# Work of the weight-decode stage moved from GpSimd to VectorE and ScalarE

## The chip, the cores and the metric

The kernel runs on one core of one Trainium2 chip. Its engines are TensorE (PE in the profile, with its weight loads as PEld), VectorE (DVE), ScalarE (ACT), GpSimd (POOL) and SyncE (SP), which issues the DMAs. The metric is the device time of one execution in microseconds, taken as the median of several runs; lower is better.

## What is computed

Windowed attention over 8 batches, 8 heads, 576 positions and a head size of 64, followed by a feed-forward layer whose activation is a rational function. The inputs are float32, except the two weight matrices, which are float64.

```
scores = q @ k.T / 8, kept where 0 <= pos_q - pos_k < 64, else -1e9
attn   = exp(scores - max) / (sum + 1e-9)
x      = attn @ v                      # 4608 tokens x 512
h      = x @ w_in                      # 512 x 2048
P      = a0 + a1*h + a2*h^2 + a3*h^3
Q      = 1 + |b0|*|h| + |b1|*h^2
out    = (P / (Q + 1e-6)) @ w_out      # 2048 x 512
```

The weights reach the kernel as pairs of 32-bit words (a low and a high word). The kernel makes float32 numbers of them itself.

## The kernel before

**Precision.** Each operand of the feed-forward matmuls is split into a high part in a reduced format (fp32r) and a low part, the rest. A product is then three matmuls: high x low, low x high, high x high. For every operand there is thus a cast for the high part and a subtraction for the low part.

**Weights.** `decode` (L101) handles one block of 128 x 512 numbers, and there are 16 blocks of `w_in` and 16 of `w_out`. It loads the word pairs into the landing buffer `w_st` (two buffers), then works in `w_c` (two buffers): L113 removes the sign of the high word (a bitwise and), L114 clamps from below, L116 shifts and masks, L117 joins the low word's upper bits, L118 joins the sign. These five run on VectorE. ScalarE casts the result to the high part (L121), and GpSimd subtracts to get the low part (L122).

**Attention.** A chunk is 384 tokens, and there are 12. For each chunk four units (one per pair of heads) run: `unit_load`, `unit_scores` (matmuls L182, mask and scale on VectorE L188 or L192, row maximum L198, six exponentials on ScalarE L201, sums and reciprocal L203 and L204, and the multiplication of all 128 x 768 numbers by the reciprocals, L205, on GpSimd), `unit_transpose` and `unit_av`, which splits the result into `xh` (ScalarE) and `xl` (VectorE, L229).

**Feed-forward.** `ffn1` (L234) does one step: 12 matmuls into the PSUM tile `h` (two buffers), then the gate, one rational function on 128 x 384 numbers. ScalarE takes |h| (L244) and a3*h + a2 (L245); VectorE makes the numerator (L246, L247); GpSimd makes the denominator less one, first the scaling u = |b1|*|h| + |b0| (L248), then the product with |h| (L249); ScalarE takes a logarithm and an exponential for the reciprocal (L251, L252); VectorE refines it and multiplies (L253 to L255); ScalarE casts to the high part `gh` (L258); the low part `gl` (L260) is a subtraction, on GpSimd for the first 20 gates (`GLN`) and on VectorE after that. `ffn2` (L270) follows three steps later with 9 matmuls.

**Order.** There are 192 steps. The first 32 are chunks 0 and 1 in halves: the first eight blocks of columns for chunk 0, then for chunk 1, then the other eight for chunk 1 and for chunk 0. The decodes are spread over the prologue and steps 0 to 22 (L304 to L315), so that a weight block is decoded some steps ahead of its use. From step 32 on each chunk takes 16 steps and no weights are decoded. The four units of chunk 2 are issued at steps 21 to 28 in the program, the eight of chunks 0 and 1 ahead of that. A planner that simulates the engines then puts the instructions of each engine into their final order, so an instruction can run well ahead of its step in the program. Each engine works its queue in order.

Of the kernel before, what the change touches and what calls it, by code (L numbers as in the profile page):

```python
# [9 lines left out]
F32 = mybir.dt.float32  # L10
F32R = mybir.dt.float32r
U32 = mybir.dt.uint32
AF = mybir.ActivationFunctionType
ALU = mybir.AluOpType
# [3 lines left out]
CH = 384  # L18
TC = CH // WIN
PR = TC // 2  # L20
GLN = 20
AHEAD = 3
LAG = 3
W_AT = 0, 1, 2, 3
# [7 lines left out]
def swa_rational_ffn(ctx: ExitStack, tc: tile.TileContext, qT, kT, v, w_in, w_out, a, b, out):  # L32
    nc = tc.nc
    P = 128
# [18 lines left out]
    op = ctx.enter_context(tc.tile_pool(name="op", bufs=2))  # L53
# [28 lines left out]
    b_sb = const.tile([P, 2], F32, name="b_sb")  # L82
# [18 lines left out]
    def decode(src, hi, lo):  # L101

        w = stage.tile([P, 512, 2], U32, name="w_st", bufs=2)
        if len(src.shape) == 3:
            nc.sync.dma_start(out=w.rearrange("p (c n) two -> p c (n two)", c=src.shape[1]), in_=src)
        else:
            nc.sync.dma_start(out=w.rearrange("p n two -> p (n two)"), in_=src)
        low, high = w[:, :, 0], w[:, :, 1]
        c = stage.tile([P, 512], U32, name="w_c")
        cf = c.bitcast(F32)  # L110


        nc.vector.tensor_scalar(out=c, in0=high, scalar1=0x7FFFFFFF, scalar2=None, op0=ALU.bitwise_and)  # L113
        nc.vector.tensor_scalar(out=cf, in0=cf, scalar1=2.0 ** -15, scalar2=None, op0=ALU.max)  # L114

        nc.vector.tensor_scalar(out=c, in0=c, scalar1=3, scalar2=0x3FFFFFF8, op0=ALU.logical_shift_left, op1=ALU.bitwise_and)  # L116
        nc.vector.scalar_tensor_tensor(out=c, in0=low, scalar=29, in1=c, op0=ALU.logical_shift_right, op1=ALU.bitwise_or)  # L117
        nc.vector.scalar_tensor_tensor(out=c, in0=high, scalar=0xC0000000, in1=c, op0=ALU.bitwise_and, op1=ALU.bitwise_or)  # L118
        if len(hi.shape) == 3:
            cf = cf.rearrange("p (c n) -> p c n", c=hi.shape[1])  # L120
        nc.scalar.copy(out=hi, in_=cf)  # L121
        nc.gpsimd.tensor_tensor(out=lo, in0=cf, in1=hi.bitcast(F32), op=ALU.subtract)  # L122

    def load_w_in(i):
        sl = slice(i * P, (i + 1) * P)
        decode(w_in_v[:, :, 2 * i * P:2 * (i + 1) * P], wi_h[:, :, sl], wi_l[:, :, sl])

    def load_w_out(i):
        decode(w_out_v[:, i, :], wo_h[:, i, :], wo_l[:, i, :])
# [42 lines left out]
    def unit_scores(c, hp):  # L172
        u = live[c, hp]

        ps = ps_a.tile([P, 2, 512], F32, name="ps_s", bufs=1)
        for p in range(PR):
            for z in range(2):
                for e in range(2):
                    j = 2 * p + e
                    k = u["kt"][z * 64:z * 64 + 64].rearrange("p t s -> p (t s)")  # L180
                    w = u["kw"][j] * WIN
                    nc.tensor.matmul(ps[e * 64:e * 64 + 64, z, p * P:(p + 1) * P], u["q"][z * 64:z * 64 + 64, j, :],  # L182
                                     k[:, w:w + P], start=True, stop=True)
        sm = att.tile([P, 2, PR * P], F32, name="sm")
        m0 = u["m0"]
        for z in range(2):
            if m0 is None:
                nc.vector.scalar_tensor_tensor(out=sm[:, z, :].rearrange("p (r c) -> p r c", c=P),  # L188
                                               in0=ps[:, z, 0:PR * P].rearrange("p (r c) -> p r c", c=P), scalar=SCALE,
                                               in1=mask[:, 1:2, :].broadcast_to([P, PR, P]), op0=ALU.mult, op1=ALU.min)  # L190
            else:
                nc.vector.scalar_tensor_tensor(out=sm[:, z, :], in0=ps[:, z, 0:PR * P], scalar=SCALE,  # L192
                                               in1=mask[:, m0:m0 + PR, :].rearrange("p r c -> p (r c)"),
                                               op0=ALU.mult, op1=ALU.min)
        sm = sm.rearrange("p z (r c) -> p (z r) c", c=P)
        NR = 2 * PR
        nmx = att.tile([P, NR], F32, name="nmx")
        nc.vector.tensor_reduce(out=nmx, in_=sm, axis=AX.X, op=ALU.max, negate=True)  # L198
        sums = att.tile([P, NR], F32, name="sums")
        for j in range(NR):  # L200
            nc.scalar.activation(sm[:, j, :], sm[:, j, :], AF.Exp, bias=nmx[:, j:j + 1], accum_out=sums[:, j:j + 1])  # L201
        rs = att.tile([P, NR], F32, name="rs")
        nc.vector.tensor_scalar(out=sums, in0=sums, scalar1=1e-9, scalar2=None, op0=ALU.add)  # L203
        nc.vector.reciprocal(out=rs, in_=sums)  # L204
        nc.gpsimd.tensor_tensor(out=sm, in0=sm, in1=rs.unsqueeze(2).broadcast_to([P, NR, P]), op=ALU.mult)  # L205
        u["sm"] = sm

    def unit_transpose(c, hp):
# [23 lines left out]
    n_gates = [0]  # L232

    def ffn1(c, i):  # L234
        h = ps_h.tile([P, CH], F32, name="h")
        n = 0
        for cc in range(NCC):
            for w, x in ((wi_h, xl), (wi_h, xh), (wi_l, xh)):
                nc.tensor.matmul(h, w[:, cc, i * P:(i + 1) * P], x[c, cc], start=n == 0, stop=n == 3 * NCC - 1)  # L239
                n += 1  # L240
        ah = tmp.tile([P, CH], F32, name="ah")
        u = tmp.tile([P, CH], F32, name="u")
        num = tmp.tile([P, CH], F32, name="num")
        nc.scalar.activation(ah, h, AF.Abs)  # L244
        nc.scalar.activation(num, h, AF.Identity, scale=a_sb[:, 3:4], bias=a_sb[:, 2:3])  # L245
        nc.vector.tensor_tensor(out=num, in0=num, in1=h, op=ALU.mult)  # L246
        nc.vector.scalar_tensor_tensor(out=num, in0=num, scalar=a_sb[:, 1:2], in1=h, op0=ALU.add, op1=ALU.mult)  # L247
        nc.gpsimd.tensor_scalar(out=u, in0=ah, scalar1=b_sb[:, 1:2], scalar2=b_sb[:, 0:1], op0=ALU.mult, op1=ALU.add)  # L248
        nc.gpsimd.tensor_tensor(out=u, in0=u, in1=ah, op=ALU.mult)  # L249

        nc.scalar.activation(ah, u, AF.Ln, bias=QADD)  # L251
        nc.scalar.activation(ah, ah, AF.Exp, scale=-1.0)  # L252
        nc.vector.scalar_tensor_tensor(out=u, in0=u, scalar=QADD, in1=ah, op0=ALU.add, op1=ALU.mult)  # L253
        nc.vector.scalar_tensor_tensor(out=u, in0=u, scalar=2.0, in1=ah, op0=ALU.subtract, op1=ALU.mult, reverse0=True)  # L254
        nc.vector.scalar_tensor_tensor(out=num, in0=num, scalar=a_sb[:, 0:1], in1=u, op0=ALU.add, op1=ALU.mult)  # L255
        gh = gp.tile([P, CH], F32R, name="gh")
        gl = gp.tile([P, CH], F32R, name="gl")
        nc.scalar.copy(out=gh, in_=num)  # L258
        n_gates[0] += 1
        (nc.gpsimd if n_gates[0] <= GLN else nc.vector).tensor_tensor(out=gl, in0=num, in1=gh.bitcast(F32), op=ALU.subtract)  # L260
        gs[c, i] = gh, gl


# [56 lines left out]
    for c, i0, i1 in phases:  # L320
        if c and c not in start:
            start[c] = s
            every = prev // NU
            for k in range(NU):
                p = max(s - prev + every * k - AHEAD, 0)
                at(p, unit_load, c, k)
                at(p, unit_scores, c, k)
                at(p + 1, unit_transpose, c, k)
                at(p + 1, unit_av, c, k)
        prev = i1 - i0  # L330
        s += prev


    for k in range(NU + 2):
        if k < NU:
            unit_load(0, k)
            unit_scores(0, k)
        if 1 <= k <= NU:
            unit_transpose(0, k - 1)
        if k >= 2:  # L340
            unit_av(0, k - 2)
        if k in W_AT:
            load_w_in(W_AT.index(k))
        if k == 1:
            load_coefficients()

    for s in range(total + LAG):
        for fn, *args in todo.get(s, ()):
            if fn in (load_w_in, load_w_out):
                fn(*args)  # L350
        if s < total:
            ffn1(*steps[s])
        for fn, *args in todo.get(s, ()):
            if fn not in (load_w_in, load_w_out):
                fn(*args)
        if s >= LAG:
            ffn2(s - LAG)
# [31 lines left out]
```

## Time and profile before

| | |
|---|---|
| median of 3 runs | 1064.74 us (1063.88 to 1066.21) |
| the profiled execution's own time | 1063.77 us |
| its span, first to last instruction | 1062.0 us |
| mean granted TensorE clock | 0.966 |
| busy: PE, DVE, ACT, POOL | 963.7, 917.7, 674.3, 525.0 us |
| weight decodes | 32, the last one ending on VectorE at 207.5 us |
| gates started by then | 17 of 192 |

Busy time is the time in which at least one instruction of an engine is under way. The profile's granted clock is the share of the full TensorE clock that the chip let through. A group of instructions is named by its line, its engine, its operation, and the tile that it writes and those that it reads. "Idle before" is the engine's idle time ahead of instructions of that group, with what ended it.

### The profile page before, as it was taken

To read this page: it belongs to the slowest core of one execution; us is meant where nothing else is said; L and a number is where in the kernel's file an instruction comes from. 1 tells how busy PE (TensorE), PEld (TensorE's weight loads), DVE (VectorE), ACT (ScalarE), POOL (GpSimd) and SP (SyncE) were. 2 spreads that over 40 slices of the span, in tenths; PEclk is the share of its full clock that TensorE was granted. 3 is DMA by queue.
4 is the path that set the end of the run, shared out by engine and by line. 5 is a ranking of instruction groups with operands and counts; after the bars stand their busy time and mean duration, and the time that the engine had idled before them with its cause. 6 is when DMAs were issued, how large, how long until landed. Compare 5 with 4: busy or idle time off the path is not lost.

```text
span 1062.0 us, 18218 instructions
## 1 busy us (share of the span) xinstructions
PE 963.7 (91%) x6624; PEld 846.0 (80%) x6624; DVE 917.7 (86%) x1583; ACT 674.3 (63%) x1702; POOL 525.0 (49%) x511
## 2 busy tenths in 40 slices
PE   2558667899999999999999999999999999999997
PEld 2446555778888888888888888888888888888996
DVE  6999989988888898898888888888888888888885
ACT  3454445467666766766766766766666667667654
POOL 5356658864454445435435535534444444454432
PEclk9778779899999999999999999999999999999999
DMA  5543343102121121110211211210211211200000
GB/s 183 173 152 93 107 130 110 35 1 73 48 66 30 59 58 32 63 61 28 70 45 29 69 48 33 92 31 28 85 29 30 88 30 32 93 16 1 31 2 30
DMA packets 68538, 64.10 MB, mean 60 GB/s; under 512 B 4448, under 2 KB 61792, under 8 KB 68448
## 3 DMA queue, kind: packets, MB, share of 16 engines
q1 hardware_dynamic: 68448, 62.93, 19.0%
q8 instruction: 52, 0.85, 0.3%
q14 instruction: 38, 0.31, 0.1%
HBM read 53.48 MB, written 9.44 MB: 59 GB/s over the span
## 4 chain that ended last, share of the span: by engine, by line
DVE 36%; ACT 20%; POOL 19%; PE 17%; issue 5%; DMA 3%; POOLq 0%; SPq 0%; DVEq 0%; ACTq 0%
PE o L280 8%; ACT sm L201 8%; POOL u L248 7%; PE h L239 7%; DVE u L253 7%; POOL u L249 6%; POOL sm L205 4%; DVE u L254 4%; DVE nmx L198 4%; DVE num L255 2%; ACT ah L251 2%; DVE w_c L117 2%; DVE gl L260 2%; ACT ah L252 2%; DVE w_c L118 2%
## 5 line engine op out<-in xcount | busy, mean ns | idle before, releaser
L239 PE MATMUL h<-xl,wi_h 128*128 128x384 f32 x768 | 269.4, 351 | 30.3 <-DVE num L247 22.3
L248 POOL TENSOR_SCALAR u<-ah,b_sb 128x384 f32<-128x384 f32 x192 | 164.6, 860 | 262.8 <-ACT ah L244 199.6
L239 PE MATMUL h<-xh,wi_h 128*128 128x384 f32 x768 | 264.3, 344 | 0.0
L239 PE MATMUL h<-xh,wi_l 128*128 128x384 f32 x768 | 263.5, 343 | 0.0
L280 PE MATMUL o<-wo_h,gl 128*128 128x512 f32 x576 | 236.8, 411 | 25.4 <-DVE gl L260 14.4
L280 PE MATMUL o<-wo_h,gh 128*128 128x512 f32 x576 | 228.6, 397 | 0.0
L280 PE MATMUL o<-wo_l,gh 128*128 128x512 f32 x576 | 228.0, 396 | 0.0
L249 POOL TENSOR_TENSOR u<-u,ah 128x384 f32<-128x384 f32 x192 | 204.5, 1071 | 9.8
L239 PEld LDWEIGHTS h<-xl,wi_h 128*128 128x128 f32 x768 | 148.2, 193 | 40.1 <-DVE num L247 26.1
L205 POOL TENSOR_TENSOR sm<-sm,rs 128x768 f32<-128x768 f32 x48 | 81.4, 1696 | 195.8 <-DVE rs L204 195.8
L201 ACT ACTIVATE sm<-sm,nmx 128x128 f32<-128x128 f32 x288 | 111.9, 390 | 102.7 <-DVE nmx L198 102.4
L260 DVE TENSOR_TENSOR gl<-num,gh 128x384 fp32r<-128x384 f32 x172 | 154.0, 899 | 13.0 <-ACT gh L258 10.0
L245 ACT ACTIVATE num<-h,a_sb 128x384 f32<-128x384 f32 x192 | 128.5, 670 | 45.7 <-DVE gl L260 35.8
L280 PEld LDWEIGHTS o<-wo_h,gl 128*128 128x128 f32 x576 | 109.6, 190 | 58.9 <-DVE gl L260 19.2
L239 PEld LDWEIGHTS h<-xh,wi_h 128*128 128x128 f32 x768 | 148.5, 193 | 4.7
L253 DVE SCALAR_TENSOR_TENSOR u<-u,ah 128x384 f32<-128x384 f32 x192 | 116.7, 608 | 40.9 <-ACT ah L252 39.2
L251 ACT ACTIVATE ah<-u 128x384 f32<-128x384 f32 x192 | 100.4, 523 | 80.2 <-POOL u L249 79.3
L239 PEld LDWEIGHTS h<-xh,wi_l 128*128 128x128 f32 x768 | 148.3, 193 | 0.0
L280 PEld LDWEIGHTS o<-wo_h,gh 128*128 128x128 f32 x576 | 109.7, 190 | 25.2
L258 ACT CAST gh<-num 128x384 fp32r<-128x384 f32 x192 | 96.7, 508 | 47.5 <-DVE num L255 47.4
L280 PEld LDWEIGHTS o<-wo_l,gh 128*128 128x128 f32 x576 | 109.9, 191 | 18.7
L255 DVE SCALAR_TENSOR_TENSOR num<-num,a_sb,u 128x384 f32<-128x384 f32 x192 | 121.1, 636 | 2.9
(45 smaller groups left out, 1274.1 us busy)
## 6 DMA issues: line engine op xcount, KB each, us to landing
out<-ob SPq DMA_DIRECT2D x33, 256.0 KB, 2.0
w_st<-w_in SPq DMA_DIRECT2D x16, 512.0 KB, 3.7
w_st<-w_out SPq DMA_DIRECT2D x16, 512.0 KB, 3.6
q<-qT SPq DMA_DIRECT2D x32, 192.0 KB, 3.4
vt<-v SPq DMA_DIRECT2D x16, 384.0 KB, 3.4
vt<-v SPq DMA_DIRECT2D x16, 320.0 KB, 3.3
kt<-kT SPq DMA_DIRECT2D x16, 224.0 KB, 3.5
kt<-kT SPq DMA_DIRECT2D x16, 192.0 KB, 3.5
```

What stands on the lines that cost most here:

```text
L201: nc.scalar.activation(sm[:, j, :], sm[:, j, :], AF.Exp, bias=nmx[:, j:j + 1], accum_out=sums[:, j:j + 1])
L205: nc.gpsimd.tensor_tensor(out=sm, in0=sm, in1=rs.unsqueeze(2).broadcast_to([P, NR, P]), op=ALU.mult)
L239: nc.tensor.matmul(h, w[:, cc, i * P:(i + 1) * P], x[c, cc], start=n == 0, stop=n == 3 * NCC - 1)
L245: nc.scalar.activation(num, h, AF.Identity, scale=a_sb[:, 3:4], bias=a_sb[:, 2:3])
L248: nc.gpsimd.tensor_scalar(out=u, in0=ah, scalar1=b_sb[:, 1:2], scalar2=b_sb[:, 0:1], op0=ALU.mult, op1=ALU.add)
L249: nc.gpsimd.tensor_tensor(out=u, in0=u, in1=ah, op=ALU.mult)
L251: nc.scalar.activation(ah, u, AF.Ln, bias=QADD)
L253: nc.vector.scalar_tensor_tensor(out=u, in0=u, scalar=QADD, in1=ah, op0=ALU.add, op1=ALU.mult)
L255: nc.vector.scalar_tensor_tensor(out=num, in0=num, scalar=a_sb[:, 0:1], in1=u, op0=ALU.add, op1=ALU.mult)
L258: nc.scalar.copy(out=gh, in_=num)
L260: (nc.gpsimd if n_gates[0] <= GLN else nc.vector).tensor_tensor(out=gl, in0=num, in1=gh.bitcast(F32), op=ALU.subtract)
L280: nc.tensor.matmul(acc[c][t], g[:, ts], w[:, i, :], start=first and n == 0, stop=last and n == 2)
```

## The change

Up to the end of decoding, and a little beyond, five kinds of work leave GpSimd: the low part of the weights goes to VectorE (L122), and so does the low part of all gates (the first 20 were on GpSimd); the scaling of the first 28 gates goes to ScalarE and their product to VectorE; the softmax multiplication of chunks 0 and 1 goes to VectorE. In return the sign removal of the decode goes from VectorE to ScalarE, as an absolute value of the high word read as a float32. Gates from the 29th on, and the softmax multiplication from chunk 2 on, stay on GpSimd.

```diff
-GLN = 20
+DEC = 28
...
-        nc.vector.tensor_scalar(out=c, in0=high, scalar1=0x7FFFFFFF, scalar2=None, op0=ALU.bitwise_and)
+        nc.scalar.activation(cf, w.bitcast(F32)[:, :, 1], AF.Abs)
...
-        nc.gpsimd.tensor_tensor(out=lo, in0=cf, in1=hi.bitcast(F32), op=ALU.subtract)
+        nc.vector.tensor_tensor(out=lo, in0=cf, in1=hi.bitcast(F32), op=ALU.subtract)
...
-        nc.gpsimd.tensor_tensor(out=sm, in0=sm, in1=rs.unsqueeze(2).broadcast_to([P, NR, P]), op=ALU.mult)
+        (nc.vector if c < 2 else nc.gpsimd).tensor_tensor(out=sm, in0=sm, in1=rs.unsqueeze(2).broadcast_to([P, NR, P]), op=ALU.mult)
...
-        nc.gpsimd.tensor_scalar(out=u, in0=ah, scalar1=b_sb[:, 1:2], scalar2=b_sb[:, 0:1], op0=ALU.mult, op1=ALU.add)
-        nc.gpsimd.tensor_tensor(out=u, in0=u, in1=ah, op=ALU.mult)
+        n_gates[0] += 1
+        if n_gates[0] <= DEC:
+            nc.scalar.activation(u, ah, AF.Identity, scale=b_sb[:, 1:2], bias=b_sb[:, 0:1])
+            nc.vector.tensor_tensor(out=u, in0=u, in1=ah, op=ALU.mult)
+        else:
+            nc.gpsimd.tensor_scalar(out=u, in0=ah, scalar1=b_sb[:, 1:2], scalar2=b_sb[:, 0:1], op0=ALU.mult, op1=ALU.add)
+            nc.gpsimd.tensor_tensor(out=u, in0=u, in1=ah, op=ALU.mult)
...
-        n_gates[0] += 1
-        (nc.gpsimd if n_gates[0] <= GLN else nc.vector).tensor_tensor(out=gl, in0=num, in1=gh.bitcast(F32), op=ALU.subtract)
+        nc.vector.tensor_tensor(out=gl, in0=num, in1=gh.bitcast(F32), op=ALU.subtract)
```

## Prediction

> **What bounds the kernel now.** I read the head of the page first, then the busy time of the engines by stretch, cut where the last weight decode ends on VectorE, then VectorE's waits, and last its groups of instructions in the decode stage.
>
> ```profile
> span 1062.0 us, 18218 instructions
> ```
>
> The last line of the last decode, from the instructions in order of time (start and duration first):
>
> ```profile
> 206.50 1.04 DVE L118 SCALAR_TENSOR_TENSOR w_c<-w_st,w_c 128x512 uint32<-128x512 uint32 x1
> ```
>
> The columns of the next view, busy time by stretch, are the length, then PE, PEld, DVE, ACT and POOL busy with counts, the granted clock, the DMA share and GB/s.
>
> ```profile
> 0.00:8.00 8.00, 1.56 (x24) 1.18 (x24) 0.00 (x0) 1.28 (x1) 6.56 (x26) 1.00 0.70 213
> 8.00:207.60 199.60, 127.87 (x861) 106.05 (x862) 189.66 (x300) 94.78 (x257) 122.97 (x93) 0.82 0.39 120
> 207.60:300.00 92.40, 89.91 (x593) 77.67 (x593) 80.97 (x136) 59.97 (x143) 46.76 (x46) 1.00 0.16 50
> 300.00:1000.00 700.00, 688.28 (x4877) 611.29 (x4876) 602.02 (x1069) 483.98 (x1235) 328.53 (x323) 1.00 0.15 47
> ```
>
> The span has two halves with different limits. From 207.6 us on TensorE is busy 97 to 98% of the time and nothing on another engine is worth much. From 8 to 207.6 us, the stage in which the 32 weight blocks are decoded, VectorE is busy 189.66 of 199.60 us and idle for only 9.94, while TensorE has 72 us to spare and ScalarE 105. GpSimd is busy 122.97 us there.
>
> ```profile
> DVE w_c L113 <- DMA w_st<-w_in: 12.7, 3, 8.1
> DVE w_c L113 <- DMA w_st<-w_out: 1.5, 2, 0.9
> DVE w_c L113 <- POOL wo_l L122: 1.4, 1, 1.4
> DVE w_c L113 <- POOL wi_l L122: 1.2, 1, 1.2
> ```
>
> These are all of VectorE's longer waits up to 207.6 us (total, times, longest); the 8.1 us is the first load. So VectorE's own queue sets the end of this stage, and the rest of the kernel follows when it lets go. The question is what its instructions cost. Its groups in the stretch 8 to 207.6 us (busy us, mean ns, idle before):
>
> ```profile
> L118 DVE SCALAR_TENSOR_TENSOR w_c<-w_st,w_c 128x512 uint32<-128x512 uint32 x32 | 33.0, 1035 | 0.1
> L117 DVE SCALAR_TENSOR_TENSOR w_c<-w_st,w_c 128x512 uint32<-128x512 uint32 x32 | 30.6, 959 | 0.3
> L114 DVE TENSOR_SCALAR w_c<-w_c 128x512 f32<-128x512 f32 x32 | 20.8, 648 | 0.3
> L116 DVE TENSOR_SCALAR w_c<-w_c 128x512 uint32<-128x512 uint32 x32 | 19.9, 621 | 0.3
> L113 DVE TENSOR_SCALAR w_c<-w_st 128x512 uint32<-128x512 uint32 x32 | 18.4, 574 | 16.7 <-DMA w_st<-w_in 12.7 <-DMA w_st<-w_out 1.5 <-POOL wo_l L122 1.4
> L253 DVE SCALAR_TENSOR_TENSOR u<-u,ah 128x384 f32<-128x384 f32 x16 | 14.2, 888 | 0.0
> L254 DVE SCALAR_TENSOR_TENSOR u<-u,ah 128x384 f32<-128x384 f32 x16 | 13.1, 830 | 0.0
> L255 DVE SCALAR_TENSOR_TENSOR num<-num,a_sb,u 128x384 f32<-128x384 f32 x16 | 11.5, 730 | 0.0
> ...
> L198 DVE TENSOR_REDUCE nmx<-sm 128x6 f32<-128x768 f32 x10 | 9.4, 942 | 0.0
> L246 DVE TENSOR_TENSOR num<-num,h 128x384 f32<-128x384 f32 x17 | 9.2, 540 | 0.0
> L192 DVE SCALAR_TENSOR_TENSOR sm<-ps_s,mask 128x384 f32<-128x384 f32 x16 | 8.1, 546 | 0.0
> ```
>
> And single instructions in order of time, VectorE's and then the one GpSimd instruction of that stretch (start, duration):
>
> ```profile
> 88.51 0.61 DVE L247 SCALAR_TENSOR_TENSOR num<-num,a_sb,h 128x384 f32<-128x384 f32 x1
> 89.03 1.14 DVE L116 TENSOR_SCALAR w_c<-w_c 128x512 uint32<-128x512 uint32 x1
> 90.09 0.55 DVE L253 SCALAR_TENSOR_TENSOR u<-u,ah 128x384 f32<-128x384 f32 x1
> 90.56 0.41 DVE L113 TENSOR_SCALAR w_c<-w_st 128x512 uint32<-128x512 uint32 x1
> 90.90 0.68 DVE L117 SCALAR_TENSOR_TENSOR w_c<-w_st,w_c 128x512 uint32<-128x512 uint32 x1
> 91.50 0.55 DVE L254 SCALAR_TENSOR_TENSOR u<-u,ah 128x384 f32<-128x384 f32 x1
> 91.97 0.41 DVE L114 TENSOR_SCALAR w_c<-w_c 128x512 f32<-128x512 f32 x1
> 92.31 0.68 DVE L118 SCALAR_TENSOR_TENSOR w_c<-w_st,w_c 128x512 uint32<-128x512 uint32 x1
> 92.91 0.60 DVE L255 SCALAR_TENSOR_TENSOR num<-num,a_sb,u 128x384 f32<-128x384 f32 x1
> ```
>
> ```profile
> 88.88 1.01 POOL L260 TENSOR_TENSOR gl<-num,gh 128x384 fp32r<-128x384 f32 x1 [1.97 <-ACT gh L258]
> ```
>
> While GpSimd runs its L260, VectorE's L116 takes 1.14 us; once GpSimd is quiet the same shape takes 0.41 (L113, L114), the two-input lines 0.68 (128x512) and 0.55 or 0.60 (128x384). The group means lie far above these. But L246 and L192, with one input in PSUM, and the reduce L198, with one input, keep 0.54, 0.55 and 0.94 us through the same stage. So the stretch comes from GpSimd, and it hits single-input scalar operations from SBUF to SBUF and operations with two inputs in SBUF. In the quiet rows the next start comes 0.07 to 0.08 us before the last end, so the net price on a full queue is 0.34 (0.41), 0.60 (0.68) and 0.47 (0.55).
>
> **The change part by part**, on VectorE's queue between 8 and 207.6 us, for the same work (32 decodes, 16 to 17 gates, 10 attention units).
>
> *What GpSimd's silence gives.* Mean minus quiet duration, per decode: L113 0.16, L114 0.24, L116 0.21, L117 0.28, L118 0.355, together 1.25 us; 32 of them are 39.9 us. Per gate: L253 0.34, L254 0.28, L255 0.13, together 0.74; 16 are 11.9. Sum 51.8 us.
>
> *What VectorE loses and gets.* The rows for the counts and the neighbours' prices:
>
> ```profile
> L121 ACT CAST wo_h<-w_c 128x512 fp32r<-128x512 f32 x16 | 9.9, 616 | 24.2 <-DVE w_c L118 24.2
> ```
>
> ```profile
> L245 ACT ACTIVATE num<-h,a_sb 128x384 f32<-128x384 f32 x17 | 11.4, 672 | 6.0 <-POOL gl L260 6.0
> ```
>
> ```profile
> L248 POOL TENSOR_SCALAR u<-ah,b_sb 128x384 f32<-128x384 f32 x17 | 22.0, 1293 | 10.7 <-DVE num L255 5.4 <-ACT wi_h L121 3.7 <-ACT ah L244 1.7
> ...
> L260 POOL TENSOR_TENSOR gl<-num,gh 128x384 fp32r<-128x384 f32 x16 | 20.9, 1309 | 10.3 <-ACT gh L258 10.3
> L249 POOL TENSOR_TENSOR u<-u,ah 128x384 f32<-128x384 f32 x17 | 20.4, 1201 | 0.7
> L205 POOL TENSOR_TENSOR sm<-sm,rs 128x768 f32<-128x768 f32 x10 | 16.1, 1610 | 11.8 <-DVE rs L204 11.8
> ```
>
> L113 goes to ScalarE: 32 x 0.34 = 10.9 us off. The low parts of the weights (L122) come: two SBUF inputs of 128x512, as L117, 32 x 0.60 = 19.2. The gates' low part (L260): 16 x 0.47 = 7.5, as L254. The product of L249: 17 x 0.47 = 8.0. The softmax scaling of chunks 0 and 1 (L205), eight units of 128x768: VectorE shows no such instruction, so its price lies between the reduce of the same size (0.94, net 0.86) and 768/512 of L117 (0.90); I take 0.86, 6.9 us. Together 41.6 on, 10.9 off: plus 30.7.
>
> *What stays on GpSimd.* Ten units of L205 ran before 207.6 us and only eight belong to chunks 0 and 1; two of chunk 2 remain, 3.2 us. GpSimd's 122.97 us cost VectorE 51.8, or 0.42 us each, so 1.4 us of the relief is not had.
>
> VectorE's queue thus gets 51.8 - 30.7 - 1.4 = 19.7 us shorter.
>
> *ScalarE* gets 32 sign removals (unknown with a step of two words: between L121's 0.616 and twice that; I take 0.616, since the cast has the same size) and 17 scalings like L245 (0.672): 19.7 + 11.4 = 31.1 us on top of 94.78, 126 of some 183. It is not the bound, even at twice the first price (146).
>
> *Waits.* Four hand-overs are new to VectorE: the clamp L114 behind ScalarE's sign removal, the low part behind the cast L121, the product behind the scaling, the gates' low part behind the cast L258. Behind each of them the whole VectorE queue stands, which the planner fills with other work. Against that the hand-over to GpSimd (1.4 + 1.2 us) goes, and ScalarE and VectorE do in 0.67 + 0.55 what GpSimd did in 1.29 + 1.20 (L248, L249). From below, all 9.94 us of idle time could go; from above the price is that of the slower rival. The nearest row is the present idle time, and I add 3 us to it.
>
> *Transfers.* No DMA is moved. SP's loads of w_st wait for L118 as before and come earlier with it; the DMA share of 0.39 leaves room. Sign removal reads the landing buffer too, but ahead of L118, so it frees nothing later.
>
> *After the stage*, gates 17 to 27 keep the product on VectorE (11 x 0.47 = 5.2 us) and the scaling on ScalarE (7.4). TensorE hides this: VectorE idles 11.4 us of that stretch of 92.4, ScalarE 32. Without that cover it costs up to 5.2; TensorE's own gap, 2.5, is the most that can be won there.
>
> **A rule that speaks against the change.** The Trainium skill, page "Perfetto Trace Analysis", section "Optimizing Scalar/DVE Operations", says that where VectorE is saturated, moving work to ScalarE or even GpSimd can pay, though between VectorE and GpSimd it may not help. Followed by its first half, adding work to a queue that is 95% busy loses those 30.7 us; its second half is what these rows show. The sum by its first half is the rival of the saturated queue below, which is worked out from rows alone.
>
> **Sum.** 19.7 - 3 = 16.7 us. The profiled execution took 1063.77 us (span 1062.0 and 1.8 around it), so it becomes 1047.1; the median of the three runs, 1064.74, becomes 1048.0.
>
> **The rivals.**
>
> *The load ring decides (slower).*
>
> ```profile
> w_st<-w_in SPq DMA_DIRECT2D x16, 512.0 KB, 3.7
> ```
>
> A load takes 3.7 us to land and there are two landing buffers, each free only after L118. Now a late load holds ScalarE's queue at the sign removal, with the gates' steps queued behind it, and VectorE then lacks decodes and gates alike. If every pair of loads exposes one landing, 16 x 3.7 = 59 us of idle time come: 1064.7 - 19.7 + 59 = 1104. It makes the kernel slower from 19.7/31 = 0.64 us for each later load. For it: the loads already cause most of VectorE's waits. Against it: of 31 later loads four exposed 6.1 us in all, and the stage would still last longer than 16 x 3.7 us by far.
>
> *A saturated queue (slower).* If the stretch weren't GpSimd's doing, only the 30.7 us would remain: 1095. The quiet rows speak against it, so it gets little.
>
> *The hand-overs eat the gain.* If each of the 49 decodes and gates exposes half of a cast (0.616) on VectorE, 15 us come back beside the 19.7: 1060; at 19.7/49 = 0.40 us each nothing is left. For it: every new wait is on one and the same engine, whose queue is in order too. Against it: ScalarE has a third of its time free.
>
> *More is won.* If idle time falls to nothing and TensorE's gap closes: 19.7 + 9.9 + 2.5 = 32.1, 1033. For it: a gate's chain gets shorter, and TensorE's clock of 0.82 in that stage may rise.
>
> *The change doesn't do what it says.* Two units of L205 remain on GpSimd in the stage; that is in the sum.
>
> **How the numbers follow.** Forecast, 1040 to 1056: 0.58. More is won, 1030 to 1040: 0.14, and 0.02 below it. Hand-overs eat most, 1056 to 1062.6: 0.10; no change, 1062.6 to 1066.9 (0.2%, about what a measurement of this kernel can tell): 0.06. Slower: 0.10 (load ring 0.08, saturated queue 0.02). Faster 0.84, same 0.06, slower 0.10. The range 1031 to 1063 leaves out 0.03 below and 0.16 above.
>
> **What would show it.** Right: the last L118 starts near 190 us and not 206.5; in the decode stage L114 and L116 mean 0.42, L117 and L118 0.68 to 0.72, L253 and L254 0.55; GpSimd has only the mask, two or three units of L205 and nothing else there; VectorE stays above 90% busy; from there on TensorE is as full as before. Wrong: two-input means that stay above 0.8 us; waits of L114 for ScalarE's sign removal or for w_st of more than 15 us in total; an order on VectorE's queue in which the low part stands right behind its cast; a later stretch longer than 855 us.

## The result, and the profile after

The changed kernel takes 1040.07 us (1037.89 to 1041.01, four runs) against 1065.47 us of the kernel before in the same runs: 0.976 of it, with a 95% interval of 0.974 to 0.978. The forecast was 1048.0 with a range of 1031 to 1063; the gain is 25.4 us where 16.7 were forecast. The time lies inside that range, at the lower edge of the likeliest part of it, 1040 to 1056.

The busy time by stretch of the changed kernel, cut where its last L118 has ended (columns as before: length, PE, PEld, DVE, ACT, POOL, granted clock, DMA share, GB/s):

```profile
8.00:202.70 194.70, 135.71 (x952) 113.36 (x953) 183.97 (x371) 136.39 (x342) 8.70 (x5) 0.89 0.42 126
202.70:300.00 97.30, 96.97 (x661) 84.96 (x660) 86.52 (x161) 69.24 (x170) 30.85 (x30) 1.00 0.16 51
300.00:1000.00 700.00, 688.44 (x4842) 611.93 (x4841) 601.59 (x1068) 481.33 (x1215) 327.19 (x324) 1.00 0.15 46
```

GpSimd's 122.97 us in the decode stage have shrunk to 8.70. VectorE is still the full engine there, with 183.97 of 194.70 us. But the stage is only 4.9 us shorter, and the kernel 25. VectorE's groups in that stage show why:

```profile
L118 DVE SCALAR_TENSOR_TENSOR w_c<-w_st,w_c 128x512 uint32<-128x512 uint32 x32 | 21.8, 685 | 0.1
L117 DVE SCALAR_TENSOR_TENSOR w_c<-w_st,w_c 128x512 uint32<-128x512 uint32 x32 | 21.8, 684 | 0.1
L114 DVE TENSOR_SCALAR w_c<-w_c 128x512 f32<-128x512 f32 x32 | 13.4, 421 | 15.6 <-ACT w_c L113 15.5
L116 DVE TENSOR_SCALAR w_c<-w_c 128x512 uint32<-128x512 uint32 x32 | 13.3, 419 | 0.1
L258 DVE SCALAR_TENSOR_TENSOR u<-u,ah 128x384 f32<-128x384 f32 x20 | 12.8, 646 | 0.0
...
L251 DVE TENSOR_TENSOR u<-u,ah 128x384 f32<-128x384 f32 x21 | 11.6, 552 | 0.0
L122 DVE TENSOR_TENSOR wo_l<-w_c,wo_h 128x512 fp32r<-128x512 f32 x15 | 11.1, 737 | 0.2
L264 DVE TENSOR_TENSOR gl<-num,gh 128x384 fp32r<-128x384 f32 x20 | 11.0, 551 | 1.3 <-ACT gh L263 1.3
L122 DVE TENSOR_TENSOR wi_l<-w_c,wi_h 128x512 fp32r<-128x512 f32 x16 | 10.9, 682 | 0.9 <-ACT wi_h L121 0.8
...
L246 DVE TENSOR_TENSOR num<-num,h 128x384 f32<-128x384 f32 x20 | 10.8, 545 | 0.0
L198 DVE TENSOR_REDUCE nmx<-sm 128x6 f32<-128x768 f32 x11 | 10.4, 947 | 0.0
...
L205 DVE TENSOR_TENSOR sm<-sm,rs 128x768 f32<-128x768 f32 x8 | 7.6, 953 | 0.1
```

L118 fell from 1.035 to 0.685 us, L117 from 0.959 to 0.684, L114 from 0.648 to 0.421, L116 from 0.621 to 0.419; L246 and L198 stayed. (The gate's scaling on ScalarE, L248 of before, is L250 now and its product on VectorE, L249 of before, L251; for the gates that stay on GpSimd the two are L253 and L254. L253 to L255 of before are L258 to L260, L258 is L263, L260 is L264.) The counts tell where the rest went: 32 decodes as before, but 20 or 21 gates in place of 16 or 17, and 11 attention units in place of 10. The planner puts four more gates ahead of the last decode. What counts is the progress of the whole program, so from here on I measure at gate 32, counted from 0, the first of chunk 2, by the start of its L245. ScalarE's instructions in order of time, of before and of the changed kernel:

```profile
283.68 0.67 ACT L245 ACTIVATE num<-h,a_sb 128x384 f32<-128x384 f32 x1
```

```profile
258.41 0.67 ACT L245 ACTIVATE num<-h,a_sb 128x384 f32<-128x384 f32 x1
```

The changed kernel is 25.3 us ahead there, and stays so: both take 78.5 us for a chunk (gate 80 to gate 96: 518.4 to 596.9, and 493.1 to 571.6), and at the last gate the lead is 25.5. All of the gain is made before chunk 2. The busy time by stretch up to that gate, of before and of the changed kernel (columns as before):

```profile
0.00:283.68 283.68, 203.01 (x1351) 170.49 (x1351) 254.80 (x408) 146.33 (x382) 167.04 (x156) 0.87 0.33 102
0.00:258.41 258.41, 192.98 (x1348) 163.11 (x1349) 233.20 (x464) 178.69 (x441) 24.92 (x40) 0.91 0.37 112
```

VectorE runs 56 instructions more there (8 softmax multiplications, 28 products and 20 low parts of gates; the 32 low parts of the weights replace the 32 sign removals) in 21.6 us less. Its idle time falls from 28.9 to 25.2 us, and the two make the 25.3.

### The profile page after: what moved, and what is told of

It reads as the page before. It is cut to its first block, busy times and chain, and to the rows that moved or that the text cites. A ratio compares the mean times of both kernels' runs of the same rounds, so it can differ in the third digit from the quotient of the medians.

```text
span 1038.0 us, 18200 instructions
## 1 busy us (share of the span) xinstructions
PE 954.8 (92%) x6624; PEld 839.2 (81%) x6624; DVE 896.2 (86%) x1639; ACT 706.8 (68%) x1762; POOL 383.4 (37%) x395
## 4 chain that ended last, share of the span: by engine, by line
DVE 33%; PE 22%; ACT 20%; POOL 16%; issue 5%; DMA 3%; POOLq 0%; SPq 0%; DVEq 0%; ACTq 0%
PE o L284 11%; PE h L239 9%; ACT sm L201 8%; POOL u L253 6%; DVE u L258 6%; POOL u L254 5%; POOL sm L205 5%; DVE nmx L198 4%; DVE u L259 3%; DVE gl L264 3%; DMA w_st<-w_in 3%; DVE num L247 2%; ACT ah L256 2%; DVE num L260 2%; DVE num L246 2%
## 5 line engine op out<-in xcount | busy, mean ns | idle before, releaser
L239 PE MATMUL h<-xl,wi_h 128*128 128x384 f32 x768 | 266.4, 347 | 24.6 <-DVE num L247 18.0
L239 PE MATMUL h<-xh,wi_h 128*128 128x384 f32 x768 | 261.5, 341 | 0.0
L239 PE MATMUL h<-xh,wi_l 128*128 128x384 f32 x768 | 260.8, 340 | 0.0
L284 PE MATMUL o<-wo_h,gl 128*128 128x512 f32 x576 | 236.7, 411 | 25.4 <-DVE gl L264 25.3
L253 POOL TENSOR_SCALAR u<-ah,b_sb 128x384 f32<-128x384 f32 x164 | 134.8, 825 | 284.2 <-ACT ah L244 172.4
L205 POOL TENSOR_TENSOR sm<-sm,rs 128x768 f32<-128x768 f32 x40 | 72.6, 1814 | 347.0 <-DVE rs L204 202.1
L264 DVE TENSOR_TENSOR gl<-num,gh 128x384 fp32r<-128x384 f32 x192 | 165.1, 864 | 15.0 <-ACT gh L263 11.9
L254 POOL TENSOR_TENSOR u<-u,ah 128x384 f32<-128x384 f32 x164 | 171.6, 1053 | 8.3
L245 ACT ACTIVATE num<-h,a_sb 128x384 f32<-128x384 f32 x192 | 128.7, 670 | 35.3 <-DVE gl L264 35.2
L258 DVE SCALAR_TENSOR_TENSOR u<-u,ah 128x384 f32<-128x384 f32 x192 | 111.1, 579 | 36.0 <-ACT ah L257 35.8
L284 PEld LDWEIGHTS o<-wo_l,gh 128*128 128x128 f32 x576 | 110.3, 191 | 19.5
L246 DVE TENSOR_TENSOR num<-num,h 128x384 f32<-128x384 f32 x192 | 105.0, 547 | 21.9 <-ACT num L245 21.8
L263 ACT CAST gh<-num 128x384 fp32r<-128x384 f32 x192 | 96.7, 508 | 36.6 <-DVE num L260 36.6
```

The costliest lines, as they stand in the source:

```text
L205: (nc.vector if c < 2 else nc.gpsimd).tensor_tensor(out=sm, in0=sm, in1=rs.unsqueeze(2).broadcast_to([P, NR, P]), op=ALU.mult)
L264: nc.vector.tensor_tensor(out=gl, in0=num, in1=gh.bitcast(F32), op=ALU.subtract)
L284: nc.tensor.matmul(acc[c][t], g[:, ts], w[:, i, :], start=first and n == 0, stop=last and n == 2)
```

## The experiments

My theory: GpSimd's accesses to SBUF stretch VectorE's, VectorE's queue bounds the decode stage, and the change trades 52 us of stretch for 31 us of work. Rivals: the planner's new order made the gain; or the shorter hand-overs did. The times, each against runs of the kernel before made beside it, and what two points of the trace say (the start of gate 32 and the length of a chunk, gate 80 to 96, in us):

| kernel | time, us | against before (95%) | gate 32 | chunk |
|---|---|---|---|---|
| before | 1065.47 | | 283.7 | 78.5 |
| changed | 1040.07 | 0.976 (0.974 to 0.978) | 258.4 | 78.5 |
| e1 chunk 2 too | 1078.03 | 1.013 (1.011 to 1.014) | 253.7 | 83.0 |
| e2 = e1 + reads on GpSimd | 1132.02 | 1.063 (1.062 to 1.065) | 308.3 | 83.0 |
| e3 = e1 + writes on GpSimd | 1084.09 | 1.018 (1.016 to 1.019) | 259.8 | 83.0 |
| e4 sign back on VectorE | 1061.56 | 0.997 (0.996 to 0.998) | 270.3 | 79.4 |
| e5 weights' low part back | 1047.45 | 0.983 (0.982 to 0.985) | 268.8 | 78.5 |
| e6 denominator back | 1046.50 | 0.983 (0.981 to 0.984) | 265.1 | 78.5 |
| e7 gates' low part back | 1048.91 | 0.985 (0.983 to 0.986) | 265.4 | 78.5 |
| e8 softmax back | 1039.57 | 0.976 (0.975 to 0.977) | 259.0 | 78.5 |
| e9 three units of chunk 2 | 1037.97 | 0.974 (0.973 to 0.976) | 256.6 | 78.6 |
| e10 e9, until gate 24 | 1036.82 | 0.974 (0.972 to 0.975) | 256.3 | 78.6 |

### e1, e2, e3: the same order with and without a busy GpSimd

```diff
# e1
-        (nc.vector if c < 2 else nc.gpsimd).tensor_tensor(out=sm, ...
+        (nc.vector if c < 3 else nc.gpsimd).tensor_tensor(out=sm, ...
# e2, beside e1, at the end of decode
+        [nc.gpsimd.tensor_tensor(out=s3, in0=hi.bitcast(F32), in1=hi.bitcast(F32), op=ALU.subtract) for _ in range(3)]
# e3, beside e1, at the same place
+        [nc.gpsimd.tensor_copy(out=s3[..., 0:1], in_=hi.bitcast(F32)[..., 0:1])] + [nc.gpsimd.memset(scr, 0.0) for _ in range(6)]
```

> The changed kernel with the softmax multiplication of chunk 2 on VectorE as well (four more units), so that GpSimd has nothing at all on SBUF before the 29th gate. Theory (VectorE's queue bounds the decode stage and GpSimd's accesses stretch it): two or three units add 0.86 us each to VectorE and take 1.8 us of GpSimd's time away, so 1037 to 1043 us, about the 1040 of the changed kernel. Rival (planner's order made the gain): any new order may move it by 5 us or more either way. It is the base for the next two, which have its order on every other engine.

> The kernel of e1 with work for GpSimd that nobody waits for: after each of the 32 decodes three subtractions 128x512 with two inputs in SBUF, into a scratch tile. The order of the instructions on VectorE, ScalarE, TensorE and SyncE is that of e1 to the last one. Theory (GpSimd's accesses stretch VectorE's): GpSimd is busy 96 x 1.3 = 125 us, as before the change, and costs VectorE 0.42 us for each of them, 40 to 52 us: 1080 to 1092 us; L117 and L118 go back to 0.9 to 1.05 us, L246 and L198 stay at 0.54 and 0.94. Rival 1 (the planner's order made the gain): the same order, so the same time as e1 within 3 us. Rival 2 (the gain came from shorter hand-overs without GpSimd): nobody waits for this work, so also the time of e1.

> The kernel of e1 with other work for GpSimd that nobody waits for: after each decode a copy of a few numbers (it sets the pace) and six memsets 128x512, which write SBUF and read nothing. Order on the other engines as in e1. If any access of GpSimd stretches every VectorE operation that e2 stretches: 192 x 0.53 = 102 us of GpSimd, 35 to 43 us more, 1075 to 1083. If only the single-input operations of VectorE collide with writes (L114, L116): 32 x 2 x 0.2 = 13 us at most, 1043 to 1053. If only GpSimd's reads count: 1040, as e1.

e1 missed by far: 1078, 38 us over the changed kernel. Its decode stage is faster, though: gate 32 starts at 253.71 us, 4.7 us ahead.

```profile
253.71 0.67 ACT L245 ACTIVATE num<-h,a_sb 128x384 f32<-128x384 f32 x1 [0.90 <-DVE gl L264]
```

The loss comes later. One chunk of the changed kernel and one of e1, in the view of busy time by stretch:

```profile
571.60:650.10 78.50, 77.03 (x554) 68.35 (x553) 67.78 (x120) 54.18 (x140) 36.87 (x37) 1.00 0.17 51
```

```profile
585.50:668.50 83.00, 79.28 (x554) 67.65 (x553) 70.34 (x120) 53.23 (x140) 40.06 (x37) 1.00 0.16 48
```

The same counts of instructions, at the same clock, take 4.5 us longer, and VectorE and GpSimd are each busier by some 3 us. The program text of this stage is the same; the order is not. Over their last 400 instructions (operation, tiles and shapes), VectorE's queues of the kernel before, of the changed kernel and of e5 to e10 are alike row by row, while e1's against theirs shows 290 lines of difference, counted on both sides. So the planner settles on one of several repeating orders after the decode stage, and e1 fell into a worse one.

That doesn't touch e2 and e3, which have e1's order on every engine but GpSimd. Their expected totals were built on 1040 us for e1, so what they test is the difference from e1. VectorE's groups up to 310 us, of e1, e2 and e3:

```profile
L118 DVE SCALAR_TENSOR_TENSOR w_c<-w_st,w_c 128x512 uint32<-128x512 uint32 x32 | 22.0, 689 | 0.1
...
L114 DVE TENSOR_SCALAR w_c<-w_c 128x512 f32<-128x512 f32 x32 | 13.5, 423 | 14.3 <-ACT w_c L113 14.1
L116 DVE TENSOR_SCALAR w_c<-w_c 128x512 uint32<-128x512 uint32 x32 | 13.2, 422 | 0.1
...
L122 DVE TENSOR_TENSOR wo_l<-w_c,wo_h 128x512 fp32r<-128x512 f32 x16 | 11.0, 690 | 0.2
```

```profile
L118 DVE SCALAR_TENSOR_TENSOR w_c<-w_st,w_c 128x512 uint32<-128x512 uint32 x32 | 23.4, 732 | 0.1
L122 DVE TENSOR_TENSOR wo_l<-w_c,wo_h 128x512 fp32r<-128x512 f32 x16 | 20.2, 1261 | 0.0
...
L116 DVE TENSOR_SCALAR w_c<-w_c 128x512 uint32<-128x512 uint32 x32 | 18.2, 577 | 0.1
L114 DVE TENSOR_SCALAR w_c<-w_c 128x512 f32<-128x512 f32 x32 | 18.2, 571 | 12.5 <-ACT w_c L113 12.5
L246 DVE TENSOR_TENSOR num<-num,h 128x384 f32<-128x384 f32 x33 | 17.9, 546 | 2.1 <-ACT num L245 2.1
...
L198 DVE TENSOR_REDUCE nmx<-sm 128x6 f32<-128x768 f32 x13 | 12.3, 945 | 0.0
```

```profile
L118 DVE SCALAR_TENSOR_TENSOR w_c<-w_st,w_c 128x512 uint32<-128x512 uint32 x32 | 21.7, 682 | 0.1
...
L116 DVE TENSOR_SCALAR w_c<-w_c 128x512 uint32<-128x512 uint32 x32 | 16.6, 526 | 0.1
L114 DVE TENSOR_SCALAR w_c<-w_c 128x512 f32<-128x512 f32 x32 | 16.1, 507 | 14.9 <-ACT w_c L113 14.8
...
L122 DVE TENSOR_TENSOR wo_l<-w_c,wo_h 128x512 fp32r<-128x512 f32 x16 | 10.9, 679 | 0.0
```

And GpSimd's added work, in e2 and in e3:

```profile
L122 POOL TENSOR_TENSOR scr<-wi_h 128x512 f32<-128x512 f32 x48 | 65.2, 1359 | 49.9 <-ACT wi_h L121 47.0
L122 POOL TENSOR_TENSOR scr<-wo_h 128x512 f32<-128x512 f32 x48 | 64.0, 1333 | 72.5 <-ACT wo_h L121 69.7
```

```profile
L122 POOL MEMSET scr<- 128x512 f32 x192 | 108.0, 563 | 11.1
```

The busy time up to gate 32, of e1, e2 and e3:

```profile
0.00:253.71 253.71, 189.83 (x1340) 159.42 (x1341) 232.62 (x466) 178.37 (x440) 16.75 (x37) 0.93 0.38 114
0.00:308.31 308.31, 210.01 (x1340) 175.85 (x1341) 288.93 (x466) 181.43 (x441) 145.94 (x133) 0.82 0.31 94
0.00:259.81 259.81, 189.52 (x1340) 158.81 (x1341) 238.56 (x466) 178.91 (x440) 139.42 (x261) 0.93 0.36 111
```

In e2, 129.2 us of reading work that nobody waits for move gate 32 by 54.6 us, and the time by 54.0. VectorE is busy 56.3 us longer with the same 466 instructions and idles 1.7 us less; TensorE's granted clock is lower there too (0.82 against 0.93), but VectorE's busy time alone covers the loss. The 54.6 us are 0.42 us for each microsecond of GpSimd's, the rate of the prediction, and this rules out both rivals as the cause of this part: the order is the same and there is no hand-over. The spread over the lines was off: the work follows the cast, so it hits L122 (0.69 to 1.26 us for w_out's blocks) more than L117 (0.79) and L118 (0.73), for which 0.9 to 1.05 was expected. L246 and L198 hardly move, as before the change.

In e3, 108 us of writing cost only 6.1. L118 stays at 0.68; L114 and L116 lose 0.084 and 0.104 us, and 32 of both are 6.0 us, the whole difference. The memsets did run beside the others too: 15 of L117, 13 of L118 and 28 of L122 lay beside memsets for more than half of their time and took 0.68 us all the same, while L114 and L116 took 0.55 and 0.58 there and 0.42 where no memset ran. So an access that only writes holds up single-input operations and leaves two-input ones alone. The Trainium skill, page "SBUF — State Buffer", section "SBUF: two separate sides", states just this split: VectorE's two-port mode collides with any GpSimd operation, its operations with two SBUF inputs only with one that reads. The traces agree, with 0.69, 1.26 and 0.68 us for L122 in e1, e2 and e3, if L114 and L116 are operations of that mode; no run here shows the mode itself.

e2 also prices the extra work. Its decode stage has e1's placing of the work (the changed kernel's, with the softmax units of chunk 2 on VectorE too) and a GpSimd about as busy as before the change (129 against 123 us), and gate 32 comes 24.6 us later than before the change. That was the rival of the saturated queue, put at 30.7.

### e4 to e8: one part undone at a time

```diff
# e4
-        nc.scalar.activation(cf, w.bitcast(F32)[:, :, 1], AF.Abs)
+        nc.vector.tensor_scalar(out=c, in0=high, scalar1=0x7FFFFFFF, scalar2=None, op0=ALU.bitwise_and)
# e5
-        nc.vector.tensor_tensor(out=lo, in0=cf, in1=hi.bitcast(F32), op=ALU.subtract)
+        nc.gpsimd.tensor_tensor(out=lo, in0=cf, in1=hi.bitcast(F32), op=ALU.subtract)
# e6
-        if n_gates[0] <= DEC:
+        if n_gates[0] <= 0:
# e7
-        nc.vector.tensor_tensor(out=gl, in0=num, ...
+        (nc.gpsimd if n_gates[0] <= 20 else nc.vector).tensor_tensor(out=gl, in0=num, ...
# e8
-        (nc.vector if c < 2 else nc.gpsimd).tensor_tensor(out=sm, ...
+        nc.gpsimd.tensor_tensor(out=sm, ...
```

> The changed kernel with one part undone: the sign removal is back on VectorE. Theory (VectorE's queue is the bound): 32 x 0.34 = 10.9 us more on it, while of the 15.5 us that it waits for ScalarE's sign removal some 5 go: 1044 to 1051 us. Rival (the hand-over to ScalarE, held up by late loads, costs more than it saves): 1030 to 1038.

> The changed kernel with one part undone: the low part of the weights is back on GpSimd (32 subtractions 128x512). Theory: VectorE loses 32 x 0.60 = 19.2 us of work, and GpSimd's 32 x 1.4 = 45 us cost it 0.42 each, 18.9 us: no difference, 1036 to 1044. Rival (moving work off GpSimd pays in each part): slower by 10 us or more. Rival (a saturated VectorE should give work away): faster by 10 us or more, 1030 or less.

> The changed kernel with one part undone: scaling and product of the denominator of all gates are on GpSimd. Theory: up to the last decode 20 gates take 20 x 0.47 = 9.4 us off VectorE and bring GpSimd 20 x 2.0 = 40 us (single-input and two-input), which cost VectorE 0.42 each, 17 us: slower by 5 to 10, 1045 to 1050. Rival (hand-overs): the chain of a gate gets 1.3 us longer and the queue waits, slower by more, 1055 and above.

> The changed kernel with one part undone: the low part of the first 20 gates is back on GpSimd. Theory: 20 x 0.47 = 9.4 us less on VectorE, 20 x 1.1 = 22 us of GpSimd cost it 9.2: no difference, 1036 to 1044. Rival (each part pays): slower by 5 us or more.

> The changed kernel with one part undone: the softmax multiplication of chunks 0 and 1 is back on GpSimd. Theory: 8 x 0.86 = 6.9 us less on VectorE, 8 x 1.5 = 12 us of GpSimd cost it 5: 0 to 3 us faster, 1036 to 1041. Rival (each part pays): slower by 3 us or more.

The start of gate 32 against the changed kernel, and what VectorE's busy and idle time up to there make of it (us):

| | gate 32 | VectorE busy | VectorE idle |
|---|---|---|---|
| e4 | +11.9 | +11.5 | +0.4 |
| e5 | +10.4 | +11.4 | -1.1 |
| e6 | +6.7 | +1.5 | +5.3 |
| e7 | +7.0 | +0.9 | +6.1 |
| e8 | +0.6 | +1.3 | -0.8 |

The planner orders the work anew each time, so a few microseconds of each may be its doing.

e4 agrees at gate 32 with 10.9 us more work on VectorE; its total was missed because its chunks take 79.4 us, one more worse order (104 lines of difference in the last 400 instructions). The waits are the same whoever takes the sign off: in the changed kernel L114 waits 15.5 us for ScalarE, in e4 L113 waits 16.3 for the loads.

e8 came as expected. e6 did so in its total, but not by the way I had given: VectorE's queue comes out almost even, +1.5 us where 7.6 were expected, and the rest is idle time: up to gate 32 L246 waits 6.1 us for ScalarE, 3.4 in the changed kernel, and L229 once for its cast, 2.5 us. So the right number was in part luck, and the hand-overs, the rival that I had put at 1055 and above, may have had a share in it. e5 and e7 did not come as expected: I had expected an even trade, and they are 7 to 9 us slower. For e5, VectorE's groups from 8 to 203 us show more stretch than the common rate gives:

```profile
L117 DVE SCALAR_TENSOR_TENSOR w_c<-w_st,w_c 128x512 uint32<-128x512 uint32 x32 | 27.4, 857 | 0.2
L118 DVE SCALAR_TENSOR_TENSOR w_c<-w_st,w_c 128x512 uint32<-128x512 uint32 x31 | 23.1, 745 | 0.3
L116 DVE TENSOR_SCALAR w_c<-w_c 128x512 uint32<-128x512 uint32 x32 | 19.9, 621 | 0.2
L114 DVE TENSOR_SCALAR w_c<-w_c 128x512 f32<-128x512 f32 x32 | 17.3, 542 | 13.0 <-ACT w_c L113 13.0
L260 DVE SCALAR_TENSOR_TENSOR num<-num,a_sb,u 128x384 f32<-128x384 f32 x18 | 15.1, 840 | 0.0
```

Against the changed kernel these five lines alone lose 32 x (0.173 + 0.06 + 0.202 + 0.121) + 18 x 0.23 = 22 us, more than the 19.2 us of work that left VectorE. In e7 the trade on the queue is even, as expected (+0.9 us), and the loss is idle time. Two waits are longer up to gate 32 than in the changed kernel: L122 for its cast (6.4 us, 6.1 of it one wait, against 0.8) and L246 for ScalarE (6.6 against 3.4). Whether e6 and e7 wait because of the longer hand-overs or because of the planner's order stays open.

The rate of 0.42 is thus an average and no constant. An estimate from the table, with the net prices for the work that left VectorE: in e5 31 us of stretch come with 49 us of GpSimd's work, 0.63 each; in e6 15 with 68 more, 0.22; in e7 10 with 36, 0.28.

### e9 and e10: the decode stage of e1 with the better later order

```diff
# e9
-        (nc.vector if c < 2 else nc.gpsimd).tensor_tensor(out=sm, ...
+        (nc.vector if c < 2 or (c == 2 and hp < 3) else nc.gpsimd).tensor_tensor(out=sm, ...
# e10, beside e9
-DEC = 28
+DEC = 24
```

> The changed kernel with the softmax multiplication of three of the four units of chunk 2 on VectorE (e1 moved all four). After the decode stage its instructions stand on TensorE, VectorE and ScalarE in the order of the changed kernel, and not in that of e1. Theory (e1 lost its 38 us to the order that the planner settles on after the decode stage, 83.0 us for each chunk against 78.5, and gained in the decode stage, where its gate 32 starts 4.7 us earlier): chunks of 78.5 us again, and 1034 to 1039 us. Rival (a GpSimd kept idle in the decode stage slows the later stage by itself): chunks of about 82 us, 1065 to 1078. Rival (the gain of e1's decode stage came from the fourth unit): 1040 or more.

> As e9, but the denominator returns to GpSimd from the 25th gate on, not the 29th. Theory: these four gates lie behind the last decode, where TensorE is full; the order of the later stage is the same, so within 1.5 us of e9. Rival (VectorE is still the bound at gates 24 to 27): 4 x 0.47 = 2 us less work on it, but GpSimd's 4 x 2 us cost 3: 1 to 3 us slower.

One unit less than in e1, the last 400 instructions of VectorE in the changed kernel's order, and the chunks take 78.6 us again: 1037.97 us against 1078.03. So e1's loss is the order's, and an idle GpSimd does no harm. The gain over the changed kernel is small, 0.974 against 0.976 of before with intervals that touch; e9's gate 32 is 1.8 us ahead, where e1's was 4.7. e10 is within 1.2 us of e9, as expected. Both beat the kernel before clearly, and the changed one by 2 to 3 us at the medians, which these runs can't quite tell from nothing.

## Why the prediction was right, point by point

**The bound and the stretch: right.** VectorE's queue set the end of the stage, and GpSimd stretched it: the group means fell to the quiet durations, and e2 brings the stretch back at the predicted 0.42 us for each of GpSimd's. That the rate is a constant, as the sum for the units that stay on GpSimd took it to be, e5 to e7 don't bear out.

**VectorE's queue, forecast 19.7 us shorter: right.** For equal work, the changed kernel's 183.97 us hold 3 more of L246 and L247, 4 more each of L258 to L260, L251 and L264, and one unit with its reduce and two mask steps: at the net prices 14.4 us. That leaves 169.6 against 189.66 us, 20.1 shorter, or 19.5 with the low part of the last block (0.60), which runs just after 202.7 us. The softmax multiplication, which VectorE's trace did not show, took 0.953 us (0.94 assumed).

**Idle time, 3 us more: too much.** In the stage it went from 9.94 to 10.73 us, 0.8 more; up to gate 32, where both kernels have done the same work, it fell by 3.7 us. The waits, after (total, times, longest):

```profile
DVE w_c L114 <- ACT w_c L113: 15.5, 8, 9.3
DVE gl L264 <- ACT gh L263: 1.3, 1, 1.3
DVE wi_l L122 <- ACT wi_h L121: 0.8, 2, 0.5
```

L114's 15.5 us are just over the 15 that I had named as a sign of failure, but 9.3 of them are the first load, which took 8.1 before. The hand-overs behind the casts and the scaling cost next to nothing, and the load ring did not decide.

**The end of the stage, "the last L118 starts near 190 us": wrong, and here lie the missing microseconds.**

```profile
L118 DVE SCALAR_TENSOR_TENSOR w_c<-w_st,w_c x32: 677/682/703, 12.5 to 202.0; 128x512 uint32<-128x512 uint32 x32
```

(Line L118 of the changed kernel: duration in ns, smallest, median and largest, then its first and last start in us.) I had taken the work ahead of the last decode as given. The planner did not make the decodes earlier; it put four more gates between them. These cost VectorE 14.4 us in the stage, and each saves 78.5/16 = 4.9 us later, where TensorE sets the pace: 4 x 4.9 - 14.4 = 5.2 us more, an estimate. With 20.1 - 0.8 = 19.3 for equal work this makes 24.5 us; the spans differ by 24.0. The count at gate 32 needs no such estimate: VectorE's queue is 21.6 us shorter there (19.7 forecast for the stage) and its idle time 3.7 us less (3 more forecast), so most of what was missing in the forecast is idle time. What shortened it, the order or the hand-overs, no run separates.

**What stays on GpSimd, 1.4 us: half of what it cost.** Not two but three units of chunk 2 ran on GpSimd in the stage; they start at 129.18, 155.06 and 174.89 us and take 1.71, 1.47 and 5.20 us. Beside each, one VectorE operation is stretched: L258 at 129.48 us takes 1.82 us and L258 at 155.77 takes 1.18, in place of 0.55, and L122 at 179.15 takes 1.49 in place of 0.68. Together that is 2.7 us. The third unit, GpSimd and then VectorE in order of time:

```profile
174.89 5.20 POOL L205 TENSOR_TENSOR sm<-sm,rs 128x768 f32<-128x768 f32 x1 [18.36 <-DVE rs L204]
```

```profile
177.61 0.68 DVE L117 SCALAR_TENSOR_TENSOR w_c<-w_st,w_c 128x512 uint32<-128x512 uint32 x1
178.21 0.55 DVE L251 TENSOR_TENSOR u<-u,ah 128x384 f32<-128x384 f32 x1
178.68 0.54 DVE L246 TENSOR_TENSOR num<-num,h 128x384 f32<-128x384 f32 x1
179.15 1.49 DVE L122 TENSOR_TENSOR wo_l<-w_c,wo_h 128x512 fp32r<-128x512 f32 x1
180.56 0.68 DVE L118 SCALAR_TENSOR_TENSOR w_c<-w_st,w_c 128x512 uint32<-128x512 uint32 x1
```

GpSimd's multiplication, 1.47 us at best, took 5.20 while VectorE ran one operation with SBUF inputs after the other. Behind L246, which has an input in PSUM, GpSimd came to its end (180.09), and only there did VectorE lose in this instance: its L122 took 1.49 us and not 0.68. e9, with three units of chunk 2 on VectorE, gained 1.8 us at gate 32.

**ScalarE: right as to the bound, priced a little low.** Its two new groups, from 8 to 202.7 us:

```profile
L113 ACT ACTIVATE w_c<-w_st 128x512 f32<-128x512 f32 x32 | 21.5, 673 | 32.9 <-DMA w_st<-w_in 20.2 <-DMA w_st<-w_out 7.7 <-DVE wo_l L122 1.9
L250 ACT ACTIVATE u<-ah,b_sb 128x384 f32<-128x384 f32 x22 | 15.4, 708 | 0.0
```

The sign removal with a step of two words took 0.673 us, near the lower end of the 0.616 to twice that, the scaling 0.708 (0.672 assumed), and ScalarE is busy 136 of 195 us.

**After the stage: right here, but a risk was not seen.** In the changed kernel a chunk takes 78.5 us as before. That the planner can settle on another order there was not among the rivals, and it can cost 4.5 us a chunk: e1 would have been a slower kernel for a reason that has nothing to do with the part edited.

## What to carry to other kernels

Look for operations whose mean differs between stages while their neighbours' doesn't: which ones are stretched (single-input from SBUF to SBUF, two inputs in SBUF) and which aren't (an input in PSUM, a reduce) points to the cause before any experiment, and an experiment can then test it. An engine at 95% may then get more work and still be faster, if the work comes from the one that blocks it. Where a planner sets the order, compare kernels at a fixed point of the program as well as by their total time, and look whether the untouched stage still runs at its old pace; add dummy work on an engine that nobody waits for to test a contention with the order held fixed.

## What the runs showed of the hardware that was not expected

- GpSimd's cost to VectorE depends on what it does: 0.42 us per microsecond of two-input subtractions (e2), 0.06 (6.1 of 108 us) for memsets (e3). It also depends on what VectorE runs at that moment: e5 to e7 give estimates from 0.22 to 0.63.
- The blocking goes both ways: one GpSimd multiplication of 128x768 was drawn out from 1.47 to 5.20 us by a full VectorE queue, in one instance. The same section of the Trainium skill's page "SBUF — State Buffer" says that whoever starts first keeps the shared ports for the whole instruction and the other one waits; that a stream of short VectorE instructions can hold GpSimd for several of its own lengths, the rows of that instance show.
